# A fused attention, expert and dense kernel: dense slices issued between the last experts, with every engine's order written out

## The chip, the cores and the metric

The kernel runs on one NeuronCore of a Trainium2 chip. The metric is the device time of one execution in microseconds (us). A core has a matrix engine (PE in the profile; its weight loads are PEld), a vector engine (DVE), an activation engine (ACT), a general engine (POOL) that issues the indirect transfers, and a queue engine (SP) that issues all other transfers. Each engine works through its own instructions in their order; semaphores hold an instruction until what it needs is there.

## What is computed

Three layers follow one another on 1536 tokens of width 512, all in 32-bit floats:

```python
a = softmax([local window scores, block scores])       # 2 batches, 8 heads, 768 positions
x = (a @ [v, block means of v]).reshape(1536, 512)
skip = x @ w_skip <= 0                                 # about half of the tokens
e = argmax(x @ w_gate)                                 # one of 8 experts for each other token
x[~skip] += gate * (relu(x @ w1[e]) @ w2[e])           # 512 -> 1024 -> 512
h = x @ w_in                                           # 512 -> 2048, the dense layer
g = where(h >= 1, h, where(h <= -1, 0, (h + 1)**2 / 4))
out = g @ w_out                                        # 2048 -> 512
```

## The kernel before

**Stages.** Attention and routing run first. Routing scatters the tokens into lists in device memory (`xf`), by expert; the skipped tokens lie at its head, so the first 512 rows (`EARLY`) need no expert. Then eight expert steps p = 0 to 7 run, and then the dense layer in three chunks of 512 tokens.

**An expert step.** The tokens of step p are a block of `ROOM[p]` rows: 64 for p = 0 and 6, 32 for the others, and 160 for one large expert (`BIG`, here p = 4), which is worked as a block of 32 rows and one of 128. For a block, `xs` transposes the rows on PE and copies the result on ACT; `as_` multiplies with w1 on PE (for 32 rows on four quarters of the array's columns at once, each with another quarter of the hidden values, L888) and applies relu on ACT (L890); `ts` transposes the hidden values on PE and copies them on ACT (L899); `bs` multiplies with w2 on PE (L906); `ys` adds the result into the rows on DVE, one instruction for each part of the result in PSUM (L914): four for a block of 32 rows, two for one of 64. `put` scatters the rows back on POOL. For the 128 rows the steps are `mx`, `ma`, `mt`, `mb` (L920, L229, L235, L240). PE's pipeline is ts(p), as_(p+1), xs(p+2), bs(p).

**Expert weights.** Each expert has 4 MB, loaded in four transfers by `fetch` (L129) on SP into one of four pairs of slots.

**The dense layer.** Its weights come in 16 slices f. `ff_fetch` loads the 64-bit words of a slice (1 MB, two transfers, L1012 and L1014) into one of four 8 KB buffers (pool `b8`); three DVE instructions (L1024, L1027, L1030, "bits") make floats of them; ACT rounds them to a high part (L1045, "high"); DVE forms the low part (L1046, "low"). The high part of an odd slice and the hidden values of experts share the tile tag `h`. For a chunk and slice, `mm1` is 12 matmuls of 512 columns (L1080), `act` makes g (in chunk 0 four ACT instructions, L1092 to L1095, then a DVE add, L1100, an ACT cast, L1105, and a DVE subtract, L1106), and `mm2` is 12 matmuls (L1121 to L1123). PE's order is mm1(i), mm2(i-1), mm1(i+1). In total there are 48 such pairs, 1152 matmuls. The first chunk's 512 rows come by four loads on SP (L857) into the ring of row buffers, issued during steps 4 and 5, and are transposed by `turn0` on PE (L219) and split in two parts on ACT and DVE (L224, L225).

**Order.** In attention, all engines issue as written. In the expert and dense stages of the kernel before only SP and POOL do; the order on PE, DVE and ACT is the planner's, steered by priorities (`SHIFT`) and by a work list from which `fill` takes a given number of conversion steps at given places (`FILLS`, `FFILLS`).

Of the kernel before, what the change touches and what calls it, by code (L numbers as in the profile page):

```python
# [30 lines left out]
SLOTS = (("00", "01"), ("02", "03"), ("10", "11"), ("13", "12"))  # L31
FFSLOTS = ("00", "01", "02", "03", "10", "11", "12", "13")
NRAW = 4
FILLS = ((0, 0, 0), (0, 0, 0), (0, 0, 0), (0, 0, 2), (2, 2, 2, 2), (2, 1, 1), (1, 1, 2))
LAST = 2
FFILLS = ((2, 1, 2), (2, 0, 2))
SHIFT = {'bits': 6, 'round': -57, 'act': -1, 'add': -97, 'g': 8, 'y': 18, 'x': -8, 't': 6, 'turn': 0}
YLAST = 4
PLACES = {4: 0, 5: 2, 6: 1, 7: 3}
# [3 lines left out]
def tile_net(ctx, tc, q, k, v, w_skip, w_gate, w1, w2, w_in, w_out, out):  # L43
# [12 lines left out]
    xnext = iter(xring * NT)  # L56
# [30 lines left out]
    wg = cp.tile([128, 4, 9], F32, name="wg")  # L87
    placei = cp.tile([1, 18], I32, name="placei")
# [33 lines left out]
    def fetch(p, c):  # L122

        n = 2 if c < 2 else 4
        if c % 2 == 0:
            tag = "w" + SLOTS[p % 4][c // 2]
# [5 lines left out]
    def work_list():  # L132

        def convert(f):
            for step in range(3):
                yield lambda: ff_bits(f, step)
            yield lambda: ff_round(f)

        for f in range(3):
            yield from convert(f)  # L140
            if f:
                for c in (2 * f - 2, 2 * f - 1):
                    yield lambda: st["turn0"](c)
        for f in range(3, NF):
            yield from convert(f)
            if f == YLAST:
                yield lambda: st["ylast"]()

    work = work_list()

    def fill(n):

        for _ in range(n):
            w = next(work, None)
            if w is not None:
                w()

    moves, puts = [], []

    def apart(d, xg, others=()):  # L160

        for o, x in moves:
            if x is not xg and all(x is not y for y in others):
# [14 lines left out]

    @contextmanager
    def shift(name):  # L180
        now = tc.cur_priority
        d = SHIFT.get(name, 0)
        tc.cur_priority = max(0, now + d)
        yield
        tc.cur_priority = now + (tc.cur_priority - max(0, now + d))
# [59 lines left out]
    def attention(actx):  # L245
# [579 lines left out]
        for f in range(2, NRAW):  # L825
            ff_fetch(f)
# [10 lines left out]
        late()  # L837
        fb_a(0, (2, 3))
# [6 lines left out]
        for c in range(4):  # L845
            fetch(3, c)
        get(BIG[0])
# [5 lines left out]
    reads = []  # L853

    def get_slots(c):
        xg = next(xnext)
        d = nc.sync.dma_start(out=xg.bitcast(I32), in_=xf[128 * c:128 * c + 128])  # L857
        if 128 * c < EARLY:
            apart(d, xg, reads)
            reads.append(xg)  # L860
        nc.vector.tensor_copy(out=perm[:, c:c + 1], in_=xg[:, 513:514].bitcast(I32))
        return xg


    def experts(mctx):
# [7 lines left out]
        def xs(key):  # L873
            n, xg = st["n", key], st["x", key]
            tp = ps.tile([128, 4, n], F32, tag="tp", name="tpx", bufs=3)
# [3 lines left out]
            with shift("x"):  # L879
                nc.scalar.copy(out=xT, in_=tp)  # L880
# [11 lines left out]
        def ts(key):  # L892
            h, n = st.pop(("h", key)), st["n", key] // 16
            tp = ps.tile([128, n, 128], F32, tag="tp", name="tph", bufs=3)
# [3 lines left out]
            with shift("t"):  # L898
                nc.scalar.copy(out=hT, in_=tp)  # L899
# [37 lines left out]
        more = {0: (5,), 1: (6,), 3: (7,)}  # L937

        xslot = {}

        def get_slot(c):
            xslot[c] = get_slots(c)

        def turn0(c):
# [4 lines left out]
            with shift("turn"):  # L949
                x128(xslot[c], xh[:, :, a], xl[:, :, a], ps.tile([128, 4, 128], F32, tag="tp", name="tps", bufs=3))  # L950

        st["turn0"] = turn0
        early = {p: [] for p in range(E)}
        for c in range(4):
            early[4 + c // 2].append(lambda c=c: get_slot(c))

# [339 lines left out]
```

## Time and profile before

| what | value |
| --- | --- |
| time, median of 3 runs (lowest to highest) | 488.2 us (486.65 to 488.48) |
| time of the profiled execution | 488.5 us |
| its span, first to last instruction | 486.8 us |
| mean granted clock of PE | 0.965 of full |
| PE busy | 455.6 us, 94% of the span |
| DVE busy | 273.7 us, 56% |
| ACT busy | 207.9 us, 43% |
| transfers | 77.19 MB, 159 GB/s over the span |

Times in the profile count from the first instruction. PE's busy time is modelled and runs over when matmuls are pipelined, so how fast PE goes is read from the starts of its instructions. In the rows below, "x16" after a matmul counts hardware instructions; a 32-bit float matmul is two of them. "[5.52 <-DMA x]" says that the engine was idle for 5.52 us before, and what ended it. The granted clock is shown as a share of 2.4 GHz.

### The profile page before, as it was taken

The page shows a single profiled execution, that of the slowest core. Times are in us where ns is not written, and L with a number is a line of the kernel's source. Part 1 is how long each engine was busy: PE and PEld are TensorE (multiplying, and loading weights), DVE is VectorE, ACT ScalarE, POOL GpSimd, SP SyncE. Part 2 cuts the span into 40 slices and gives each one's busy share as a digit, 9 for nine tenths or more (in the row PEclk, how much of TensorE's full clock was granted, in tenths as well). Part 3 has the DMA queues.
Part 4 walks back from the last instruction along what each step waited for, and adds up shares of the span by engine and source line. Part 5 has one row for each costly group of instructions (what it writes and reads, how often), then busy time and mean ns, then how long its engine had stood idle before and what let it go on. Part 6 is the DMA issues. An engine that isn't in the chain of part 4 may idle for free.

```text
span 486.8 us, 8032 instructions
## 1 busy us (share of the span) xinstructions
PE 455.6 (94%) x3010; PEld 332.3 (68%) x3010; DVE 273.7 (56%) x629; ACT 207.9 (43%) x418; POOL 70.6 (15%) x143
## 2 busy tenths in 40 slices
PE   6889999988979995999999999999999999999993
PEld 3567777765434341557778888888888888888882
DVE  3666575785611457599999954433334453333341
ACT  4556555451112122357767765433333443333341
POOL 7001940222330300130000000300000030000003
PEclk9999998995989999699999999999999999999998
DMA  9999999989999999444556600200000020000002
GB/s 196 198 216 194 196 174 230 376 306 374 391 365 398 385 396 380 141 140 140 183 197 224 241 1 25 86 0 1 0 2 0 1 86 0 2 0 1 0 0 94
DMA packets 77104, 77.19 MB, mean 159 GB/s; under 512 B 50606, under 2 KB 58830, under 8 KB 76672
## 3 DMA queue, kind: packets, MB, share of 16 engines
q1 hardware_dynamic: 74176, 68.33, 48.2%
q0 software_dynamic: 2880, 8.25, 4.6%
q8 instruction: 26, 0.43, 0.4%
q14 instruction: 22, 0.18, 0.1%
HBM read 69.44 MB, written 7.76 MB: 159 GB/s over the span
## 4 chain that ended last, share of the span: by engine, by line
issue 42%; PE 29%; DMA 11%; DVE 10%; POOL 5%; SPq 1%; ACT 1%; POOLq 0%; DVEq 0%; ACTq 0%
PE hf L1080 7%; DMA xf<-x,ids 5%; DMA vraw<-in_v_dram 3%; PE s L395 3%; PE o L1121 3%; PE o L1123 2%; PE o L1122 2%; POOL vraw L323 2%; PE hp L229 2%; PE xo L425 2%; POOL out_dram L1133 1%; PE yp L240 1%; PE pt L407 1%; DVE x L914 1%; SPq L303 1%
## 5 line engine op out<-in xcount | busy, mean ns | idle before, releaser
L1080 PE MATMUL hf<-xh,ffw 128*128 128x512 f32 x384 | 126.6, 390 | 0.0
L1080 PEld LDWEIGHTS hf<-xh,ffw 128*128 128x128 f32 x384 | 72.1, 188 | 16.1 <-issue 0.8
L1121 PE MATMUL o<-ffw,g 128*128 128x512 f32 x192 | 76.3, 397 | 0.1
L1122 PE MATMUL o<-ffw,g 128*128 128x512 f32 x192 | 75.5, 393 | 0.0
L1080 PE MATMUL hf<-xl,ffw 128*128 128x512 f32 x192 | 74.9, 390 | 0.0
L1123 PE MATMUL o<-ffw,g 128*128 128x512 f32 x192 | 70.2, 391 | 0.0
L1090 ACT ACTIVATE c<-c,scal 128x512 f32<-128x512 f32 x32 | 23.2, 724 | 74.5 <-DVE c L1089 72.2
L1100 DVE TENSOR_TENSOR hf<-hf,c 128x512 f32<-128x512 f32 x48 | 33.5, 698 | 37.6 <-ACT hf L1098 36.1
L1133 POOL DMA_INDIRECT out_dram<-ob,perm x12 | 11.7, 974 | 247.3 <-DVE ob L1132 162.5
L1106 DVE TENSOR_TENSOR g<-hf,g 128x512 fp32r<-128x512 f32 x48 | 33.1, 690 | 23.4 <-ACT g L1105 23.3
L1089 DVE TENSOR_SCALAR c<-hf 128x512 f32<-128x512 f32 x32 | 22.1, 692 | 40.1 <-PE hf L1080 40.1
L1105 ACT CAST g<-hf 128x512 fp32r<-128x512 f32 x48 | 28.2, 587 | 37.9 <-DVE hf L1100 37.8
L400 ACT ACTIVATE p<-s,nm 128x120 f32<-128x120 f32 x96 | 26.7, 361 | 37.1 <-DVE nm L397 19.8
L1121 PEld LDWEIGHTS o<-ffw,g 128*128 128x128 f32 x192 | 36.1, 188 | 8.8 <-ACT g L1105 1.2
L1123 PEld LDWEIGHTS o<-ffw,g 128*128 128x128 f32 x192 | 36.0, 188 | 8.6 <-DVE g L1106 0.3
L1080 PEld LDWEIGHTS hf<-xl,ffw 128*128 128x128 f32 x192 | 36.1, 188 | 7.5
L1122 PEld LDWEIGHTS o<-ffw,g 128*128 128x128 f32 x192 | 36.1, 188 | 7.0
L914 DVE SCALAR_TENSOR_TENSOR x<-yp,x 32x512 f32<-32x512 f32 (+1 forms) x28 | 20.8, 744 | 10.5 <-PE yp L906 9.6
L395 PE MATMUL s<-pb 64*64 64x120 f32 x384 | 25.7, 275 | 0.0
L397 DVE TENSOR_REDUCE nm<-s 128x4 f32<-128x480 f32 x24 | 15.7, 653 | 15.4 <-PE s L395 12.4
L395 PEld LDWEIGHTS s<-pb 64*64 64x64 f32 x384 | 20.1, 136 | 5.4 <-issue 5.4
L1045 ACT CAST ffw<-cv 128x1024 fp32r<-128x1024 f32 x16 | 16.6, 1046 | 13.3 <-DVE cv L1030 11.4
(221 smaller groups left out, 643.4 us busy)
## 6 DMA issues: line engine op xcount, KB each, us to landing
w<-in_moe_w_dram SPq DMA_DIRECT2D x32, 1024.0 KB, 15.3
raw<-in_moe_w_in_dram SPq DMA_DIRECT2D x16, 512.0 KB, 4.2
raw<-in_moe_w_out_dram SPq DMA_DIRECT2D x16, 512.0 KB
x<-xf SPq DMA_DIRECT2D x12, 264.0 KB, 5.2
raw<-in_k_dram SPq DMA_DIRECT2D x16, 192.0 KB
raw<-in_q_dram SPq DMA_DIRECT2D x16, 192.0 KB, 5.0
vraw<-in_v_dram SPq DMA_DIRECT2D x4, 768.0 KB, 7.8
vw<-in_v_dram SPq DMA_DIRECT2D x13, 192.0 KB, 6.2
```

Source lines behind the costliest of these rows:

```text
L395: nc.tensor.matmul(s[a, u], tq[a, j], tk[a, j], start=False, stop=u == 3)
L400: nc.scalar.activation(out=p[:, u], in_=s[:, u], func=AF.Exp, bias=nm[:, u:u + 1], scale=1.0)
L914: nc.vector.scalar_tensor_tensor(out=xg[0:n, 0:512], in0=yp[a], scalar=xg[0:n, 512:513], in1=xg[0:n, 0:512], op0=ALU.mult, op1=ALU.add)
L1080: nc.tensor.matmul(hp, w[:, 128 * kk:128 * kk + 128], a[:, kk], start=(n == 0), stop=(n == 11))
L1089: nc.vector.tensor_scalar(out=c, in0=hp, scalar1=-1.0, scalar2=1.0, op0=ALU.max, op1=ALU.min)
L1090: nc.scalar.activation(out=c, in_=c, func=AF.Square, bias=half, scale=0.5)
L1100: nc.vector.tensor_tensor(out=hp, in0=hp, in1=c, op=ALU.add)
L1105: nc.scalar.copy(out=gh, in_=hp)
L1106: nc.vector.tensor_tensor(out=gl, in0=hp, in1=gh.bitcast(F32), op=ALU.subtract)
L1121: nc.tensor.matmul(ops[ch][t], gh[:, a], hi, start=(f == 0), stop=False)
L1122: nc.tensor.matmul(ops[ch][t], gh[:, a], lo, start=False, stop=False)
L1123: nc.tensor.matmul(ops[ch][t], gl[:, a], hi, start=False, stop=(f == NF - 1))
```

## The change

- The large expert moves from step 4 to step 5 (`BIG`, `ROOM`, `PLACES`, `SLOTS`).
- The first 512 rows come by one load into a `b8` buffer, issued on SP after the routing and before the weights of step 3 (`get_rows`); a second small transfer takes the 512 output places. The loads of raw slices 2 and 3, which stood before the weights of step 3, move back: slice 2 to step 1, slice 3 to step 4.
- `bs` puts the four parts of a 32-row block in two places of PSUM instead of four, and `ys` adds two parts instead of four.
- The indices of `put` have twelve columns of their own instead of four rotating buffers.
- Slices 0 and 1 are converted in step 3, and the first chunk's rows are turned in step 4, where the first mm1 also goes. Five dense slices' mm1 and four mm2 are issued between steps 4 and 7; weights of steps 6 and 7 are loaded between the raw slices.
- In the expert and dense stages every engine issues in the order of the text (`manual_schedule()` without an argument); `feed` becomes a generator that stops after mm1 and `act`, after `split`, and after mm2.

```diff
-BIG = (4,)
-ROOM = (64, 32, 32, 32, 160, 32, 64, 32)
+BIG = (5,)
+ROOM = (64, 32, 32, 32, 32, 160, 64, 32)
...
-        ids = cp.tile([128, 1], I32, tag="ids", name="ids", bufs=4)
+        ids = next(putids)
...
-        for f in range(2, NRAW):
-            ff_fetch(f)
...
         late()
+        get_rows()
...
+    def get_rows():
+
+        t = st["rows"] = b8.tile([128, 4, 512], F32, tag="b8", name="rows")
+        v = xf[0:EARLY].rearrange("(t p) c -> p t c", p=128)
+        for out, c in ((t.bitcast(I32), slice(0, 512)), (perm[:, 0:4].unsqueeze(2), slice(513, 514))):
+            d = nc.sync.dma_start(out=out, in_=v[:, :, c])
+            apart(d, t)
+
...
-            for c in range(n // 16):
+            m = n // 16
+            for c in range(m):
                 for f, a in enumerate(sides(n)):
-                    nc.tensor.matmul(yp[a], hT[:, c, a], wx[p, 1][:, n // 16 * f + c], start=c == 0, stop=c == n // 16 - 1)
+                    nc.tensor.matmul(yp[sides(n)[f % 2]], hT[:, c, a], wx[p, 1][:, m * f + c], start=c == 0 and f < 2,
+                                     stop=c == m - 1 and f >= 128 // n - 2)
             st["y", key] = yp
 
...
-            with shift("y"):
-                for a in sides(n):
-                    nc.vector.scalar_tensor_tensor(out=xg[0:n, 0:512], in0=yp[a], scalar=xg[0:n, 512:513],
-                                                   in1=xg[0:n, 0:512], op0=ALU.mult, op1=ALU.add)
+            for a in sides(n)[0:2]:
+                nc.vector.scalar_tensor_tensor(out=xg[0:n, 0:512], in0=yp[a], scalar=xg[0:n, 512:513],
+                                               in1=xg[0:n, 0:512], op0=ALU.mult, op1=ALU.add)
             put(key)
...
+        big = BIG[0]
         xs(0)
         as_(0, 0)
         xs(1)
         st.pop("beyond")()
-        for p in range(E - 1):
-            last = p + 2 == E
+        for p in range(big):
             ts(p)
-            if p in BIG:
-                mt((p, 1))
+            if p < 2:
+                fetch(p + 4, 0), fetch(p + 4, 1)
             if p:
                 ys(p - 1)
-                if p - 1 in BIG:
-                    put((p - 1, 1))
-            for o in more.get(p, ()):
-                get(o)
-            if p + 4 < E:
-                fetch(p + 4, 0), fetch(p + 4, 1)
-            n = iter(FILLS[p])
-            fill(next(n))
+            if p in (1, 2):
+                get(p + 5)
+            if p == 3:
+                convert(0)
+                convert(1)
+            if p == 4:
+                turn0(0), turn0(1)
+                bs(4, 4)
+                turn0(2), turn0(3)
+                st.pop("rows")
+                ff_fetch(3)
+                for c in range(4):
+                    fetch(6, c)
+                ys(4)
+                g = feed()
+                next(g), next(g), next(g)
+                ff_fetch(4)
             as_(p + 1, p + 1)
-            fill(next(n))
-            if p + 1 in BIG:
+            if p + 1 == big:
                 for f in range(2):
-                    ma((p + 1, 1), p + 1, f)
-            for f in early[p]:
-                f()
-            if not last:
-                xs(p + 2)
-                if p + 2 in BIG:
-                    mx((p + 2, 1))
+                    ma((big, 1), big, f)
+                break
+            xs(p + 2)
+            if p + 2 in BIG:
+                mx((p + 2, 1))
             bs(p, p)
-            if last:
-                ys(p)
-                ts(p + 1)
-            fill(next(n))
-            if p in BIG:
-                mb((p, 1), p)
-                if last:
-                    put((p, 1))
-                fill(next(n))
-            if p + 4 < E:
+            if p < 2:
                 fetch(p + 4, 2), fetch(p + 4, 3)
-            if p == E - 2:
-                ff_fetch(NRAW), ff_fetch(NRAW + 1)
-        bs(E - 1, E - 1)
-        st["ylast"] = lambda: ys(E - 1)
-        fill(LAST)
+            if p == 1:
+                ff_fetch(2)
+        ts(big)
+        mt((big, 1))
+        xs(6)
+        convert(2)
+        bs(big, big)
+        mb((big, 1), big)
+        convert(3)
+        ys(big)
+        put((big, 1))
+        ff_fetch(5)
+        fetch(7, 0), fetch(7, 1)
+        st["late"] = "h"
+        next(g)
+        as_(6, 6)
+        next(g)
+        next(g)
+        ts(6)
+        bits(4)
+        ff_fetch(6)
+        fetch(7, 2), fetch(7, 3)
+        high(4), low(4)
+        next(g)
+        bs(6, 6)
+        xs(7)
+        next(g)
+        ys(6)
+        next(g)
+        bits(5)
+        ff_fetch(7)
+        next(g)
+        as_(7, 7)
+        next(g)
+        high(5), low(5)
+        next(g)
+        ts(7)
+        bits(6)
+        high(6), low(6)
+        next(g)
+        bs(7, 7)
+        next(g)
+        next(g)
+        bits(7)
+        ys(7)
+        bits(8, (0, 1))
+        st["next"], st["auto"] = 8, 1
+        for _ in g:
+            pass
 
...
-    def ff_bits(f, step):
+    def bits(f, steps=range(3)):
...
-        if step == 2:
-            raw64.pop(f)
-            if NRAW <= f < NF - 2:
-                ff_fetch(f + 2)
-
-    def ff_round(f):
+                raw64.pop(f)
+                if 5 < f < NF - 2:
+                    ff_fetch(f + 2)
+
+    def high(f):
 
         g = f // 2
...
-        nc.vector.tensor_tensor(out=lo, in0=uf, in1=hi.bitcast(F32), op=ALU.subtract)
+        nc.scalar.copy(out=ffw[g][:, f % 2, 0:4:2], in_=cv[f].bitcast(F32))
+
+    def low(f):
+
+        w = ffw[f // 2][:, f % 2]
+        nc.vector.tensor_tensor(out=w[:, 1:4:2], in0=cv.pop(f).bitcast(F32), in1=w[:, 0:4:2].bitcast(F32),
+                                op=ALU.subtract)
+
+    def convert(f):
+        bits(f), high(f), low(f)
...
+
+        def split(ch, f, hp, c, between=None):
+            nc.vector.tensor_tensor(out=hp, in0=hp, in1=c, op=ALU.add)
+            if between is not None:
+                between()
...
         for i, (ch, f) in enumerate(seq):
             hp = mm1(ch, f)
-
-            act(ch, f, hp, FFILLS[min(i, len(FFILLS) - 1)])
+            c = act(ch, f, hp)
+            yield
+            n = st.get("next", NF + 1)
+            auto = "auto" in st
+            if auto:
+                runs(n - 1, high)
+            split(ch, f, hp, c, (lambda: runs(n, lambda f: bits(f, (2,)))) if auto else None)
+            if auto:
+                runs(n - 1, low)
+                runs(n + 1, lambda f: bits(f, (0, 1)))
+                st["next"] = n + 1
+            yield
...
     with ExitStack() as mctx:
-        with tc.manual_schedule(engines={EngineType.SP, EngineType.Pool}):
+        with tc.manual_schedule():
             experts(mctx)
-            feed()
```

## Rows read from the trace of the kernel before

**Rows 1.** Engine busy time by stretches of the expert and dense stages.
```profile
core 0: us, PE busy (x) PEld busy (x) DVE busy (x) ACT busy (x) POOL busy (x), PEclk, DMA share, GB/s
138.00:142.00 4.00, 4.00 (x14) 1.22 (x12) 0.05 (x1) 0.00 (x0) 0.12 (x1) 0.57 1.02 374
...
163.00:189.00 26.00, 25.02 (x138) 10.10 (x126) 14.06 (x19) 4.51 (x9) 3.79 (x4) 1.00 1.04 391
189.00:195.00 6.00, 0.48 (x4) 0.07 (x2) 3.19 (x5) 2.59 (x3) 0.37 (x1) 0.83 0.95 347
195.00:203.00 8.00, 7.81 (x37) 4.36 (x38) 2.88 (x9) 1.91 (x5) 1.35 (x1) 0.50 0.44 136
...
210.00:283.00 73.00, 72.86 (x326) 57.45 (x325) 70.18 (x88) 52.78 (x80) 3.66 (x2) 1.00 0.54 187
283.00:478.00 195.00, 195.00 (x871) 160.75 (x870) 80.34 (x117) 75.10 (x124) 8.77 (x9) 1.00 0.04 13
```

**Rows 2.** Timeline of PE: its longest wait, and its last matmul (start, duration, instruction).
```profile
194.96 1.94 PE L219 MATMUL tps<-ident,x 128*128 128x128 f32 x8 [5.52 <-DMA x<-xf]
...
479.02 0.39 PE L1123 MATMUL o<-ffw,g 128*128 128x512 f32 x1
```

**Rows 3.** Timeline of the queue engine SP: the four loads of the first rows.
```profile
180.40 18.10 SPq L857 DMA_DIRECT2D x<-xf  x4
```

**Rows 4.** Timeline of PE through the expert steps 0 to 2.
```profile
136.64 0.79 PE L877 MATMUL tpx<-ident,x 64*128 64x64 f32 x8 [2.30 <-DMA x<-xf,re]
...
146.22 3.65 PE L906 MATMUL yp<-w,hT 128*64 128x512 f32 x16
149.80 0.44 PE L896 MATMUL tph<-ident,h 128*128 128x128 f32 x2
150.17 1.93 PE L888 MATMUL hp<-w,xT 128*32 128x256 f32 x32
152.03 0.43 PE L877 MATMUL tpx<-ident,x 32*128 32x32 f32 x4
152.39 1.92 PE L906 MATMUL yp<-w,hT 128*32 128x512 f32 x16
154.25 0.44 PE L896 MATMUL tph<-ident,h 128*128 128x128 f32 x2
```

**Rows 5.** DVE's groups, 120 to 290 us: busy, mean ns of one, idle before.
```profile
L1030 DVE SCALAR_TENSOR_TENSOR cv<-raw,cv 128x1024 int32<-128x1024 int32 x16 | 19.5, 1219 | 0.1
L1027 DVE SCALAR_TENSOR_TENSOR cv<-raw,cv 128x1024 int32<-128x1024 int32 x16 | 19.5, 1224 | 0.3
L1046 DVE TENSOR_TENSOR ffw<-cv,ffw 128x1024 fp32r<-128x1024 f32 x16 | 19.5, 1218 | 1.0 <-ACT ffw L1045 0.8 <-issue 0.2
L914 DVE SCALAR_TENSOR_TENSOR x<-yp,x 32x512 f32<-32x512 f32 x24 | 17.8, 743 | 3.6 <-PE yp L906 2.9
L1024 DVE TENSOR_SCALAR cv<-raw 128x1024 int32<-128x1024 int32 x16 | 11.0, 686 | 3.3 <-DMA xf<-x,si 2.1 <-DMA raw<-in_moe_w_out_dram 1.2
L1100 DVE TENSOR_TENSOR hf<-hf,c 128x512 f32<-128x512 f32 x14 | 9.7, 696 | 0.2
```

**Rows 6.** ACT's groups in the same stretch, in the same columns.
```profile
L1045 ACT CAST ffw<-cv 128x1024 fp32r<-128x1024 f32 x16 | 16.6, 1046 | 13.3 <-DVE cv L1030 11.4 <-PE hp L229 1.9
L1095 ACT ACTIVATE c<-c,scal 128x512 f32<-128x512 f32 x14 | 10.2, 730 | 0.1
...
L1105 ACT CAST g<-hf 128x512 fp32r<-128x512 f32 x14 | 8.2, 588 | 12.1 <-DVE hf L1100 12.1
...
L890 ACT ACTIVATE h<-hp 128x256 f32<-128x256 f32 x6 | 2.3, 384 | 18.9 <-PE hp L888 17.3 <-issue 1.6
```

**Rows 7.** Timeline of ACT around two conversions and the relu behind them.
```profile
189.45 1.99 ACT L1045 CAST ffw<-cv 128x1024 fp32r<-128x1024 f32 x2 [8.44 <-DVE cv L1030]
193.66 0.60 ACT L890 ACTIVATE h<-hp 128x512 f32<-128x512 f32 x1 [2.22 <-DVE ffw L1046]
```

**Rows 8.** PE's group of the 128-row second matmul, 136 to 210 us.
```profile
L240 PE MATMUL yp<-w,hTm 128*128 128x512 f32 x16 | 7.4, 605 | 0.0
```

**Rows 9.** The chain of waits in the dense stage: start, time on the chain, what.
```profile
290.68 0.44 PE tpf L1062 x4
...
293.89 2.73 PE hf L1080 x12
```

More of the change, by code (lines that the diff above doesn't have):

```diff
@@ L1 @@
-from contextlib import ExitStack, contextmanager
+from contextlib import ExitStack
 import concourse.bass as bass
@@ L26 @@
 NEARLY = 4
-BIG = (4,)
-ROOM = (64, 32, 32, 32, 160, 32, 64, 32)
+BIG = (5,)
+ROOM = (64, 32, 32, 32, 32, 160, 64, 32)
 LISTS = 1536
 EOFF = 28 * CAP + 8 * LISTS
[L31 to L39, printed above, removed]
+SLOTS = (("00", "01"), ("02", "03"), ("10", "11"), ("13", "12"), ("00", "01"), ("02", "03"), ("10", "11"), ("00", "01"))
+FFSLOTS = ("13", "12", "02", "03", "10", "11", "00", "01")
+XORDER = (0, 1, 2, 3, 4, 5, 6, 0, 1, 2, 3, 4, 5) + (6, 0, 1, 2, 3, 5, 4, 6, 0) + (1, 2, 3, 4, 5, 6, 0, 1)
+PLACES = {4: 2, 5: 0, 6: 1, 7: 3}
 @with_exitstack
@@ L55, in tile_net @@
     xring = [xp.tile([128, XW], F32, name=f"x{i}") for i in range(7)]
-    xnext = iter(xring * NT)
+    xnext = iter([xring[i] for i in XORDER])
     dr = ctx.enter_context(tc.tile_pool(name="dr", bufs=1, space=DRAM))
@@ L87, in tile_net @@
     wg = cp.tile([128, 4, 9], F32, name="wg")
+    idsall = cp.tile([128, 12], I32, name="ids")
+    putids = iter([idsall[:, i:i + 1] for i in range(12)])
     placei = cp.tile([1, 18], I32, name="placei")
@@ L130, in fetch, with apart @@
                           .rearrange("p e k f -> p (e k) f"))
[L132 to L156, printed above, removed]
     moves, puts = [], []
-    def apart(d, xg, others=()):
+    def apart(d, xg):
         for o, x in moves:
-            if x is not xg and all(x is not y for y in others):
+            if x is not xg:
                 tc.declare_no_dep(d.ins, o.ins, reason="the blocks have different tokens")
@@ L846, in attention @@
             fetch(3, c)
+        get(4)
         get(BIG[0])
@@ L874, in xs @@
             n, xg = st["n", key], st["x", key]
-            tp = ps.tile([128, 4, n], F32, tag="tp", name="tpx", bufs=3)
+            tp = ps.tile([128, 4, n], F32, tag=st.get("late", "tp"), name="tpx", bufs=3)
             for kk in range(4):
@@ L878, in xs @@
             st["xT", key] = xT = wk.tile([128, 4, n], F32, tag="xT", name="xT", bufs=3)
-            with shift("x"):
-                nc.scalar.copy(out=xT, in_=tp)
+            nc.scalar.copy(out=xT, in_=tp)
         def as_(key, p):
@@ L897, in ts @@
             st["hT", key] = hT = wk.tile([128, n, 128], F32, tag="hT", name="hT", bufs=3)
-            with shift("t"):
-                nc.scalar.copy(out=hT, in_=tp)
+            nc.scalar.copy(out=hT, in_=tp)
         def bs(key, p):
@@ L948, in turn0 @@
             xh, xl = xTs[0]
[L949 to L955, printed above, removed]
+            x128(st["rows"][:, c], xh[:, :, a], xl[:, :, a], ps.tile([128, 4, 128], F32, tag="tp", name="tps", bufs=3))
+        big = BIG[0]
         xs(0)
@@ L1015, in ff_fetch @@
         raw64[f] = t
-    def ff_bits(f, step):
-        if step == 0:
-            cv[f] = st["wk"].tile([128, 2, 512], I32, tag="h" if f % 2 else "cv", name="cv", bufs=2 if f % 2 else 1)
-        t, o = raw64[f], cv[f]
-        with shift("bits"):
+    def bits(f, steps=range(3)):
+        for step in steps:
+            if step == 0:
+                odd = f % 2
+                cv[f] = st["wk"].tile([128, 2, 512], I32, tag="h" if odd else "cv", name="cv", bufs=2 if odd else 1)
+            t, o = raw64[f], cv[f]
             if step == 0:
@@ L1140, in feed, with runs @@
         seq = [(ch, f) for ch in range(NC) for f in range(NF)]
+        def runs(f, *fs):
+            for g in fs:
+                g(f) if f < NF else None
         for i, (ch, f) in enumerate(seq):
             hp = mm1(ch, f)
-            act(ch, f, hp, FFILLS[min(i, len(FFILLS) - 1)])
+            c = act(ch, f, hp)
[10 more added lines that the diff above has]
+            yield
             if ch + 1 < NC:
@@ L1148, in feed @@
                 if f >= NF - 4:
-                    turn(ch + 1, f - NF + 4, range(4))
-                    parts(ch + 1, f - NF + 4)
+                    kk = f - NF + 4
+                    turn(ch + 1, kk, range(4))
+                    get_perm(4 * (ch + 1) + kk, xin[ch + 1][kk])
+                    parts(ch + 1, kk)
             if i and i + 2 < len(seq):
                 mm2(*seq[i - 1])
+            yield
         a, b, c = seq[-3:]
```

57 lines of the change are left out of this document (16 added, 41 removed).

## The prediction

> **What bounds the kernel now.** I read the busy time by stretches first, then PE's timeline, then the groups of DVE and ACT. From 210 us on PE sets the time: between 283 and 478 it is never idle and DVE is busy for 80 of 195 us; between 210 and 283 PE is still full although DVE works 70.2 of 73 [rows 1]. A dense matmul starts every 2.73 / 12 = 0.2275 us [rows 9], so 1152 take 262.1; with 32 transposes of the later chunks (0.44 for four [rows 9], 3.5 together) the dense layer costs PE 265.6 us. PE's last matmul ends at 479.4 [rows 2], and the profiled time is 488.5, so 9.1 lies behind and around. That part stays.
>
> The expert steps are PE's too. In steps 0 to 2 one instruction group follows the other without a gap [rows 4]; the transfers run at full share in that stretch, but no row there has PE waiting for a weight. The losses are elsewhere: PE stands still for 5.5 us before 194.96, until a load of the first rows lands [rows 2]; SP issued those four loads over 18.1 us [rows 3], behind the last weights. Then PE runs at half clock, 1.2 GHz, from 195 to 203 [rows 1], where 8 us do the work of 4. So 9.6 us can be won here. A smaller loss is a half-clock stretch at 138 to 142 after a wait of 2.3 us for gathered rows [rows 1, 4]; nothing in the change touches it, since the weights still fill the queues there. I take 0; were that wait to vanish with its half clock, 4.0 us would come off.
>
> **Part by part. The first rows.** Their load now stands on SP before the weights of step 3, in a time when the queue has nothing else to issue, and is used only in step 4. The 5.5 and 4.1 us go. The 1 MB moved ahead replaces 2 MB of raw slices, so the weights of steps 3 to 5 land no later. The second, small transfer has 512 pieces; nothing waits for its places until the first output, so it is hidden. Separate index columns for put cost nothing and remove waits of DVE that PE doesn't see.
>
> **bs on two places.** A 64-row block already runs eight matmuls on two places: 3.65 us. A 32-row block runs eight of the same width on four: 1.92 [rows 4]. After the change the 32-row blocks use two as well, so each bs costs PE 1.73 more; steps 1 to 5 and 7 have one. What it saves is two instructions of 0.74 on DVE [rows 5], 12 in all, 8.9 us on an engine that isn't the bound before 210. Lower bound of the price: 0, if the places didn't matter; upper bound 1.73; I take 1.7, since the two rows differ in nothing else.
>
> The Trainium skill, TensorEngine Tiling (Array Packing), section "Overview" (Theoretical Speedup), gives up to 4 times for 32 columns and up to 2 times for 64, which speaks against this edit. By it the price would be the whole of 1.92, and the sum below 0.9 us longer; the rows show a ratio of 1.9, so nearly that.
>
> **Steps 1 to 3, as written.** bs of step 0 ends at 149.8 [rows 4]; without the planner's filling some 0.5 later, at 150.3. A step is ts, as_, xs, 2.6 us (149.80 to 152.39 [rows 4]), and a bs of 3.6: steps 1 and 2 end at 156.5 and 162.7. Step 3 on PE is 2.6, the large block's transposes 0.6, and 3.6: done at 169.5. But in the text the conversions of slices 0 and 1 stand in step 3 before the relu of as_(4). DVE first does ys(2), which waits for bs(2) at 162.7: two of 0.74 and the index, 1.9 with gaps. Then, with 0.69, 1.22, 1.22 for bits, 1.22 for low [rows 5] and 1.05 for high [rows 6]: bits(0) 3.2, high(0) 1.1, low(0) 1.3, bits(1) 3.2, high(1) 1.1, relu 0.45 and a signal 0.2: ts(4) can start at 162.7 + 12.4 = 175.1. ACT has the relu queued behind high(1), and PE has ts(4), turn0 and bs(4) queued behind that relu. PE stands still for 5.6 us. The trace has this in small: a relu on ACT starts 2.2 us late behind two conversions, held until a low part is done [rows 7]. Bounds: 0, if the relu got past, and 7.3, if PE had no cover from the longer bs(3). I take 5.6.
>
> The Trainium skill, TensorE: Matmul & The Clock Gate, section "Architectural detail: the array is 16× 32×32, not 1× 128×128", calls the queues of ACT and DVE strictly first in, first out. By that rule the relu can't pass; without it this sum would be 5.6 shorter; rows 7 agree with the rule.
>
> **The clock.** Idle times of 2.3 and 5.5 us were each followed by 1.2 GHz [rows 1, 2, 4]. For 5.6 us I take 2 us of loss; the bounds are 0 and the 4.1 seen at 195.
>
> **Step 4.** From 175.1: ts 0.4, two turn0 0.9 (with the row copies still queued on ACT, to 176.5), bs(4) 3.6, two turn0 0.9: 181.0. mm1(0) needs the last low part of the rows: two casts of 0.59 and a subtract of 0.69 behind the transposes, 1.7 us in which PE waits. mm1 2.73: 185.4, and with the clock 187.4. Call that M.
>
> **After M.** PE's own work up to the end of mb is as_(5) 1.9, ma 6.9, three transposes 1.7, bs(5) 3.6, mb 6.9 (7.4 busy [rows 8] less the last one's tail): M + 21.0. Then to the first matmul of mm2(5): mm1(1) to (6) and mm2(0) to (4), 11 of 2.73, with as_(6), bs(6), as_(7), bs(7) and transposes, 43.4, and 0.3 of small waits: M + 64.7. DVE must by then have g(5). In the text convert(3) stands behind mb's addition, so bits(3) can't start before M + 21.9 although DVE is free for 7 us before. From there DVE and ACT take turns, each link behind the one before: bits(3), high(3), four activations (0.7 each [rows 6]), relu, cast, subtract to M + 31.5; bits(4), high(4), activations, add, cast, subtract to 40.9; ys(6), bits(5) to 45.8; g(3) and low(5) to 49.5; bits(6), high(6), activations, g(4) to 58.8; bits(7), ys(7), two thirds of bits(8) to 65.7; add, last third, subtract: g(5) at M + 68.4. PE waits 3.3 us in mm2(5), done at M + 70.7. Then each iteration asks DVE for an add, three bits, a low part and a subtract, 0.70 + 3.13 + 1.22 + 0.69 with gaps 5.9, against PE's 5.46: some 0.45 is lost in each of six iterations, 2.9 with the first, until the last slice is converted. The raw slices land in time: each load is issued at least 5 us before its bits. Bounds for this stage: 1.5 us, what the stage loses before (from 210 to 479.4 are 269.4 us for 265.6 and 2.3 of expert work), and 6.2; I take 6.2, because the order is fixed.
>
> **The sum.** Left after M + 70.7 are 996 matmuls, 226.6, the transposes, 3.5, and 2.9: PE ends at M + 303.7 = 491.1. With 9.1: 500.2 against 488.5; the run lies 0.3 above the median. Forecast 500.
>
> **Rivals.** *The order costs nothing.* The relu of step 4 isn't held, and DVE keeps up behind M: one mechanism, conversions that don't stand in the way of what PE needs. Then ts(4) starts at 169.5, M is 179.8, and PE ends at M + 297.5 = 477.3: 486.4, not slower. For it: DVE is busy only 14 of 26 us between 163 and 189 [rows 1], so there is room for both conversions. Against it: rows 7, and that ys(2) ties their start to bs(2). It decides from the point where high(1) is done before 169.5, 5.6 us earlier than I have it. With the 4.0 of the gathered rows it would be 482.
>
> *The places of bs cost nothing.* Then steps 1 and 2 end 3.5 earlier, bs(4) and bs(5) save 1.7 each (bs(3) and bs(7) lie under other waits): 493. The two rows of bs speak against it.
>
> *The rows come late all the same,* behind weights as now: up to 5.5 us more in step 4, 505. Against it: 12 MB of weights stand behind them, not before.
>
> **How the numbers follow.** My forecast, with its own range 494 to 504: 0.66. Free places: 0.07. Late rows or a longer half clock: 0.05. Order free, 486.4: 0.15. Order free and the gather earlier, 482: 0.07. Half a per cent, 2.4 us, is about what a measurement of this kernel can tell from no change. Slower: 0.78; same: 0.15; faster: 0.07. The range 487 to 505 leaves out the fastest case and about half of the one before it.
>
> **What would show it.** ACT's relu of step 4 some 5 us after as_(4), behind two L1045-like casts; PE idle for 5 to 6 us before the transposes of that step, and half clock after; bs of 32 rows at 3.6 us; no wait for the first rows; PE waiting on a subtract of g around the sixth slice. The forecast is wrong if PE runs through step 3, or if mm1(0) starts before 178 us.

## The result and the profile after

The changed kernel takes 494.4 us, median of 4 runs (493.9 to 497.0), against 488.3 (486.7 to 488.7) of the kernel before: 6.0 us more by the medians. The ratio over all runs is 1.0141, 95% interval 1.0105 to 1.0177, so 1.4% slower. Forecast was 500.0, slower, in a range of 487 to 505. The profiled execution is the slowest of the four, 497.0 us with a span of 495.3.

PE's timeline of the changed kernel, steps 1 to 4, answers to [rows 2, 4]. M is again the end of mm1(0), here 184.46.

```profile
150.65 3.63 PE L873 MATMUL yp<-w,hT 128*32 128x512 f32 x16
154.21 0.44 PE L863 MATMUL tph<-ident,h 128*128 128x128 f32 x2
...
160.36 0.44 PE L863 MATMUL tph<-ident,h 128*128 128x128 f32 x2
160.73 1.93 PE L855 MATMUL hp<-w,xT 128*32 128x256 f32 x32
...
163.54 3.63 PE L873 MATMUL yp<-w,hT 128*32 128x512 f32 x16
172.09 0.69 PE L863 MATMUL tph<-ident,h 128*128 128x128 f32 x2 [4.92 <-ACT h L857]
172.58 1.91 PE L182 MATMUL tps<-ident,rows 128*128 128x128 f32 x8
174.42 4.62 PE L873 MATMUL yp<-w,hT 128*32 128x512 f32 x16
178.97 1.09 PE L182 MATMUL tps<-ident,rows 128*128 128x128 f32 x8
180.79 0.50 PE L1080 MATMUL hf<-xh,ffw 128*128 128x512 f32 x1 [0.73 <-ACT xh L187]
181.63 0.50 PE L1080 MATMUL hf<-xl,ffw 128*128 128x512 f32 x1 [0.34 <-DVE xl L188]
```

No line waits for a transfer of the first rows. In its place stands an idle time of 4.92 us ahead of step 4's transposes, released by the relu (L857). A 32-row bs takes 3.63 us, where [rows 4] have 1.92. ACT's timeline says why the relu was late:

```profile
165.22 1.04 ACT L1037 CAST ffw<-cv 128x1024 fp32r<-128x1024 f32 x1 [4.01 <-DVE cv L1026]
170.71 1.04 ACT L1037 CAST ffw<-cv 128x1024 fp32r<-128x1024 f32 x1 [4.45 <-DVE cv L1026]
171.66 0.38 ACT L857 ACTIVATE h<-hp 128x256 f32<-128x256 f32 x1
```

The relu's input, the L855 group of as_(4) at 160.73, was done at 162.7. The relu began at 171.66, right behind the second of two casts, and ACT was idle for 4.01 and 4.45 us before these, waiting for DVE's bits. The windows, which answer to [rows 1], show the clock and the DVE stretch:

```profile
core 0: us, PE busy (x) PEld busy (x) DVE busy (x) ACT busy (x) POOL busy (x), PEclk, DMA share, GB/s
138.00:142.00 4.00, 3.66 (x21) 1.38 (x18) 0.00 (x0) 0.75 (x2) 1.82 (x2) 1.00 0.96 352
...
167.00:172.00 5.00, 0.17 (x2) 0.00 (x0) 3.82 (x5) 1.29 (x3) 0.21 (x1) 0.76 1.05 381
172.00:176.00 4.00, 3.90 (x14) 2.37 (x16) 3.85 (x6) 2.23 (x6) 0.89 (x1) 0.50 0.85 300
...
250.00:283.00 33.00, 32.22 (x141) 25.95 (x140) 32.69 (x38) 24.80 (x37) 0.00 (x0) 1.00 0.68 236
```

After the idle time PE runs at 1.2 GHz from 172 to 176. From 250 to 283 DVE is busy for 32.69 of 33 us, and PE still for 32.22. The wait for a part of g in mm2(5), the second matmul of the sixth slice, is short in PE's timeline:

```profile
250.89 0.50 PE L1119 MATMUL o<-ffw,g 128*128 128x512 f32 x1 [0.41 <-ACT g L1104]
251.23 0.40 PE L1120 MATMUL o<-ffw,g 128*128 128x512 f32 x1
252.00 0.50 PE L1121 MATMUL o<-ffw,g 128*128 128x512 f32 x1 [0.37 <-DVE g L1105]
```

The matmul before the first of these started at 250.09. By the starts, at 0.2275 us a matmul, the two waits are 0.57 + 0.54 = 1.1 us.

### The profile page after: what moved, and what is told of

The parts are those of the page before. It is cut to its first block, busy times and chain, and to the rows that moved or that the text cites. A ratio compares the mean times of both kernels' runs of the same rounds, so it can differ in the third digit from the quotient of the medians.

```text
span 495.3 us, 7993 instructions
## 1 busy us (share of the span) xinstructions
PE 462.0 (93%) x3010; PEld 333.0 (67%) x3010; DVE 265.3 (54%) x613; ACT 208.7 (42%) x418; POOL 68.0 (14%) x143
## 4 chain that ended last, share of the span: by engine, by line
issue 36%; PE 36%; DVE 8%; DMA 7%; SPq 4%; POOL 4%; ACT 2%; ACTq 1%; POOLq 0%; DVEq 0%
PE hf L1080 8%; PE yp L873 4%; SPq L266 3%; PE hp L855 3%; DMA w<-in_moe_w_dram 3%; PE o L1119 3%; PE o L1121 2%; PE o L1120 2%; PE s L358 2%; PE hp L192 2%; POOL vraw L286 2%; PE xo L388 2%; DMA vw<-in_v_dram 2%; DMA vraw<-in_v_dram 2%; POOL out_dram L1131 2%
## 5 line engine op out<-in xcount | busy, mean ns | idle before, releaser
L1119 PE MATMUL o<-ffw,g 128*128 128x512 f32 x192 | 76.7, 399 | 1.1 <-ACT g L1104 1.1
L1120 PE MATMUL o<-ffw,g 128*128 128x512 f32 x192 | 75.5, 393 | 0.0
L1121 PE MATMUL o<-ffw,g 128*128 128x512 f32 x192 | 75.1, 391 | 0.4 <-DVE g L1105 0.4
L1089 ACT ACTIVATE hf<-hf,scal 128x512 f32<-128x512 f32 x32 | 21.2, 662 | 85.2 <-DVE c L1088 85.2
L1131 POOL DMA_INDIRECT out_dram<-ob,perm x12 | 11.7, 974 | 229.7 <-DVE ob L1130 227.0
L873 PE MATMUL yp<-w,hT 128*32 128x512 f32 (+1 forms) x128 | 30.1, 613 | 0.0
L1037 ACT CAST ffw<-cv 128x1024 fp32r<-128x1024 f32 x16 | 16.6, 1039 | 28.3 <-DVE cv L1026 28.3
L1042 DVE TENSOR_TENSOR ffw<-cv,ffw 128x1024 fp32r<-128x1024 f32 x16 | 19.6, 1222 | 10.0 <-ACT ffw L1037 10.0
```

Of the source, the lines that this page charges most:

```text
L873: nc.tensor.matmul(yp[sides(n)[f % 2]], hT[:, c, a], wx[p, 1][:, m * f + c], start=c == 0 and f < 2, stop=c == m - 1 and f >= 128 // n - 2)
L1119: nc.tensor.matmul(ops[ch][t], gh[:, a], hi, start=(f == 0), stop=False)
L1120: nc.tensor.matmul(ops[ch][t], gh[:, a], lo, start=False, stop=False)
L1121: nc.tensor.matmul(ops[ch][t], gl[:, a], hi, start=False, stop=(f == NF - 1))
L1131: d = nc.gpsimd.indirect_dma_start(out=out[:, :], out_offset=bass.IndirectOffsetOnAxis(ap=perm[:, 4 * ch + t:4 * ch + t + 1], axis=0), in_ ...
```

## The experiments

The kernels did not all run on one chip, so each is told by its ratio to the kernel before on its own chip and its 95% interval. Within a trace, lengths are counted from ts(0), the first transposes of hidden values, since what lies ahead of it differs by some us between executions; the last section has the waits there. "Front" is ts(0) to M, "back" is M to PE's last matmul. The changed kernel has 184.46 - 141.66 = 42.8 and 488.05 - 184.46 = 303.6, together 346.4; the kernel before, in which mm1(0) comes later, has 335.6 together. Work is left out in none. No run separates the other parts of the change, above all the large expert's move and the dense slices between the experts.

| kernel | ratio (interval) | front | back | sum |
| --- | --- | --- | --- | --- |
| changed | 1.0141 (1.0105 to 1.0177) | 42.8 | 303.6 | 346.4 |
| conversions spread | 1.0014 (0.9991 to 1.0038) | 35.7 | 303.6 | 339.3 |
| four places everywhere | 1.0106 (1.0083 to 1.0129) | 39.1 | 305.8 | 344.8 |
| spread, four places in steps 1, 2 | 0.9937 (0.9915 to 0.9959) | 32.3 | 303.6 | 335.9 |
| before, rows alone | 1.0121 (1.0090 to 1.0153) | - | - | 344.8 |
| before, two places alone | 1.0105 (1.0079 to 1.0132) | - | - | 342.4 |
| changed, planner's order | 1.0405 (1.0381 to 1.0428) | 53.5 | 300.0 | 353.5 |
| all three edits | 0.9939 (0.9919 to 0.9959) | 29.3 | 305.8 | 335.1 |
| two edits behind the large expert | 1.0194 (1.0162 to 1.0226) | 43.1 | 305.1 | 348.2 |
| all three, less late DVE work | 0.9814 (0.9799 to 0.9830) | 29.2 | 301.6 | 330.8 |
| same, first mm1 covered | 0.9791 (0.9776 to 0.9807) | 29.8 | 298.5 | 328.2 |
| before, rows alone, earlier list | 1.0085 (1.0065 to 1.0106) | - | - | 341.8 |

**Conversions spread.**

```diff
+            if p in (3, 4):
+                low(p - 3)
             if p:
                 ys(p - 1)
...
-            if p == 3:
-                convert(0)
-                convert(1)
+            if p == 1:
+                bits(0)
...
+            if p == 2:
+                bits(1)
...
             bs(p, p)
+            if p in (2, 3):
+                high(p - 2)
```

> The changed kernel, with the conversions of slices 0 and 1 spread out: bits(0) in step 1, bits(1) in step 2, high(0) after bs(2), high(1) after bs(3), low(0) and low(1) behind the transposes of steps 3 and 4. Nothing else differs. Theory: in the changed kernel PE stands still for 4.92 us in step 4 because ACT's relu of that step is written behind high(1), and the stretch at half clock after it costs some 2 us more. Then both go: no idle time of over 1 us before the transposes of step 4, full clock from 165 to 180, mm1(0) at about 174.8 instead of 180.8, and 494.4 - 6.9 = 487.5 us. Rival, the order costs nothing (PE waits for something else there, as a late weight): the idle time stays or moves by a step, 494. Rival, the gain is given back in the chain of conversions behind the large expert: the end of mm1(0) comes 6 us earlier, but the wait in mm2(5) grows by some 3 us or more: 490 to 491.

The front is 7.1 us shorter, the back unchanged. PE's timeline has no idle time ahead of the transposes of step 4, and bs(4) takes 3.63 again:

```profile
164.95 0.44 PE L863 MATMUL tph<-ident,h 128*128 128x128 f32 x2
165.22 1.04 PE L182 MATMUL tps<-ident,rows 128*128 128x128 f32 x8
166.19 3.63 PE L873 MATMUL yp<-w,hT 128*32 128x512 f32 x16
```

So the hold was the position of two conversions in the text, and cost 4.9 us of waiting and 2.2 of clock. Without it the kernel is level with the kernel before: 1.0014, with 1 inside the interval. That doesn't make the hold the only cost: other costs and gains of the change cancel. In the profiled runs this kernel is 3.7 us longer than the kernel before from ts(0) on, and the kernel before lost 3.3 us more ahead of it (from the last 128-row second matmul ahead of the experts to ts(0), 143.84 - 127.23 = 16.6 us against 139.51 - 126.23 = 13.3).

**Four places everywhere.**

```diff
-                    nc.tensor.matmul(yp[sides(n)[f % 2]], hT[:, c, a], wx[p, 1][:, m * f + c], start=c == 0 and f < 2,
+                    nc.tensor.matmul(yp[a], hT[:, c, a], wx[p, 1][:, n // 16 * f + c], start=c == 0, stop=c == n // 16 - 1)
...
-            for a in sides(n)[0:2]:
+            for a in sides(n):
```

> The changed kernel with bs of a 32-row block back on four places of PSUM and ys back on four additions. Theory: two places cost PE 1.7 us for each block. Steps 1 and 2 get 3.5 us shorter, bs(3) only lengthens the idle time, ys(2) is 1.5 longer ahead of the conversions, so ts(4) starts 2.0 earlier; bs(4) is 2 shorter; behind the large expert bs(5) and bs(7) save 3.4 on PE, but ys(5) and ys(7) put 3.0 more on DVE, and the wait in mm2(5) grows from 1.1 to some 6. Sum about -2.6: 491.8 us (490 to 493). Rival, the places of bs cost nothing: bs stays at 3.6 us, and only the additions are left, +1.5 and +3.0: 498 to 499. Rival, DVE has room for the four additions everywhere: -7 and more, 487 or less.

A bs takes 1.92 on PE's timeline; the hold grows to 8.19, as DVE's chain behind ys(2) is longer and PE arrives earlier; the wait in mm2(5) grows to 3.87:

```profile
159.24 1.92 PE L872 MATMUL yp<-w,hT 128*32 128x512 f32 x16
169.35 0.69 PE L863 MATMUL tph<-ident,h 128*128 128x128 f32 x2 [8.19 <-ACT h L857]
...
246.32 0.80 PE L1117 MATMUL o<-ffw,g 128*128 128x512 f32 x1 [3.87 <-ACT g L1102]
246.92 0.63 PE L1118 MATMUL o<-ffw,g 128*128 128x512 f32 x1
```

The front gives 3.7, the back takes 2.2, so the profiled run is 1.5 shorter from ts(0) on. The ratios' intervals overlap: in this order no effect of the places can be told. PE's saving of 1.7 for each of six blocks, 10.3, comes back for the most part: 3.3 in the longer hold, of which 1.5 are additions, and 5.6 behind M, in the longer wait and what follows it. That the places are free on PE is refuted.

**Both, the places in steps 1 and 2 alone.**

```diff
+        def parts_of(key, n):
+
+            return sides(n)[0:4 if key in (1, 2) else 2]
...
-            for a in sides(n)[0:2]:
+            for a in parts_of(key, n):
```

> The changed kernel with both: the conversions of slices 0 and 1 spread over steps 1 to 4 as in the experiment before, and four places of PSUM (and four additions) for steps 1 and 2 alone, where DVE is idle. Theory: the two costs are separate and add up: -6.9 and -3.5, less what DVE's longer additions hold back the low parts of the first rows: M, the end of mm1(0), at about 173.5 instead of 184.4, and the end likewise: 483.5 us (482 to 486), faster than the kernel before. Rival, the conversions of the raw slices wait for DVE or the transfers behind the large expert: M comes early, but the wait in mm2(5) or a wait for weights of step 6 takes it back: 487 or more.

The front falls by another 3.4, twice 1.7, and the back stays: the two costs add up where DVE is idle.

**The rows alone, in the kernel before.**

```diff
-NRAW = 4
+NRAW = 3
...
-        for f in range(3):
+        for f in range(2):
             yield from convert(f)
...
+        get_rows()
...
+            if c == 3:
+                st.pop("rows")
+                ff_fetch(3)
```

> The kernel before with one part of the change alone: the first 512 rows come in one load issued behind the routing into a b8 buffer, raw slice 3 is loaded when the rows are turned, and the four turns follow slice 1 in the work list. Order on PE, DVE and ACT is still the planner's, and bs and the large expert are as before. Theory: the wait of 5.5 us for the first rows and the half clock after it, 4.1 us, go: 488.3 - 9.6 = 478.7 us; with the earlier gather that the changed kernel showed (0.84 instead of 2.30, no half clock) up to 2 less. Rival, the wait moves to what is late next (a raw slice, DVE's subtract of the rows): at least half of it stays, 483 to 485. Rival, the rows were not what held PE: 488.

None of the three expected outcomes was a loss. The wait for the rows is gone, the transposes start at 185.19 instead of 194.96 [rows 2], but PE then waits 5.76 us for a copy of hidden values. PE and ACT there:

```profile
192.21 1.12 PE L218 MATMUL tps<-ident,rows 128*128 128x128 f32 x4 [5.76 <-ACT hT L902]
```

```profile
188.92 1.99 ACT L1041 CAST ffw<-cv 128x1024 fp32r<-128x1024 f32 x2 [8.41 <-DVE cv L1026]
190.82 1.06 ACT L223 CAST xh<-tps 128x512 fp32r<-128x512 f32 x2
191.77 0.38 ACT L902 COPY hT<-tph 128x256 f32<-128x256 f32 x1
```

It is the hold of the changed kernel, a conversion ahead of what PE needs, in the planner's order. But DVE, whose bits the casts wait for, was late too:

```profile
178.05 0.15 DVE L206 SCALAR_TENSOR_TENSOR ids<-vl,x 64x1 int32<-64x1 f32 x1 [5.44 <-DMA xf<-x,ids]
```

It stood idle for 5.44 us until a scatter gave back one of `put`'s four rotating index buffers, and worked without a gap from there to the end of the bits, at 188.89. The kernel before has the same wait (5.41 us before 178.58), but there the rows come later still. The changed kernel gives `put` columns of its own; this run doesn't have them, so what the order alone costs here is not shown.

A second loss follows: at 230.67 and 232.73 mm1 waits 1.82 and 1.32 for a slice's two parts, though the transfers are idle from 214 to 230 (share 0.00); that slice's bits start at 224.57, and DVE was idle for 6.56 us before 218.28. These bits wait for no transfer. That they fall late because the rows take one of four 8 KB buffers isn't shown; the planner's order alone could do it.

**The same, with the work list taken earlier.** By the end of steps 3 and 4 four more conversion steps have been taken, after step 5 one.

```diff
-FILLS = ((0, 0, 0), (0, 0, 0), (0, 0, 0), (0, 0, 2), (2, 2, 2, 2), (2, 1, 1), (1, 1, 2))
+FILLS = ((0, 0, 0), (0, 0, 0), (0, 0, 1), (1, 2, 2), (2, 2, 2, 2), (0, 0, 1), (1, 1, 1))
```

> The run with the rows alone (planner's order, 1.012 of the kernel before), with the work list taken two items earlier in steps 2 to 4, so that slice 1 is converted before the hidden values of step 5 are copied. Theory: in the run with the rows alone the copy of step 5's hidden values stood behind two casts on ACT, 5.8 us of idle time for PE; with those casts done sooner the wait goes, and the rows give some 5 to 9 us: 0.982 to 0.99 of the kernel before. Rival, the planner lets a cast or a low part stand ahead of something else that PE needs: 1.0 or more.

The rival held: the idle time is 5.56 now, at 180.87, behind DVE's subtract of the rows, and the waits at the slice stay (1.82 and 1.33). DVE again stood idle just before, for 5.46 us up to 175.06, for an index buffer of `put`. What list would let the planner use the early rows was not found, and early rows together with index columns were not tried on this text. The planner's order of the changed text, below, has both; there DVE waits for gathers.

**The places alone, in the kernel before.**

```diff
-                    nc.tensor.matmul(yp[a], hT[:, c, a], wx[p, 1][:, n // 16 * f + c], start=c == 0, stop=c == n // 16 - 1)
+                    nc.tensor.matmul(yp[sides(n)[f % 2]], hT[:, c, a], wx[p, 1][:, m * f + c], start=c == 0 and f < 2,
...
-                for a in sides(n):
+                for a in sides(n)[0:2]:
```

> The kernel before with one part of the change alone: bs of a 32-row block on two places of PSUM, ys with two additions. Theory: 1.73 us on PE for each of six blocks. Those of steps 1 to 3 (5.2) only shorten the wait of 5.5 us for the first rows, that of the large expert's step comes half under it; the last two stand on PE's path, one of them at half clock: +4 to +6, 493 us. Rival, PE's price is paid back by the additions that DVE no longer does, since DVE works 70 of 73 us between 210 and 283: 488 (487 to 490). Rival, the places of bs cost PE nothing: 488 or a little less.

Measured 489.05 against 484.43, +4.6 by the medians (ratio 1.0105), in the expected 4 to 6. The wait for the rows falls from 5.5 to 1.76 us: it had covered the first blocks.

**The planner's order on the changed text.**

```diff
-        with tc.manual_schedule():
+        with tc.manual_schedule(engines={EngineType.SP, EngineType.Pool}):
```

> The changed kernel with the written order on SP and POOL alone; on PE, DVE and ACT the planner orders the same text. Theory: the 5 us of idle time and the 2 us at half clock belong to the order as written, where the relu of step 4 stands behind two conversions; the planner lets a relu that is ready go first: 487 to 489 us. Rival, the planner puts the conversions ahead of what PE needs as well (as it did with the hidden values' copy in the run with the rows alone): 494 or more.

The theory fell: 4% slower. The planner keeps the casts ahead of the relu, and puts a small DVE instruction of `put` for a later block ahead of everything; DVE waits for that block's gather. PE and DVE:

```profile
177.87 0.69 PE L863 MATMUL tph<-ident,h 128*128 128x128 f32 x2 [11.01 <-ACT h L857]
```

```profile
165.03 0.15 DVE L170 SCALAR_TENSOR_TENSOR ids<-vl,x 64x1 int32<-64x1 f32 x1 [10.04 <-DMA x<-xf,rl]
165.21 1.52 DVE L881 SCALAR_TENSOR_TENSOR x<-yp,x 32x512 f32<-32x512 f32 x2
172.12 0.15 DVE L170 SCALAR_TENSOR_TENSOR ids<-vl,x 32x1 int32<-32x1 f32 x1 [5.38 <-DMA x<-xf,rl]
```

So the written order as such is no loss; against this one order of the planner it is worth over 2% for this text.

**Two edits behind the large expert; all three edits.** The first moves `convert(3)` and has four places in steps 5 and 7. The second adds the spread conversions and four places everywhere, and moves ys(3) and low(1).

```diff
+            return sides(n)[0:4 if key in (5, 7) else 2]
...
         convert(2)
+        convert(3)
         bs(big, big)
         mb((big, 1), big)
-        convert(3)
```

The second, beside the spread conversions:

```diff
-            for a in sides(n)[0:2]:
+            for a in sides(n):
...
-            if p:
+            if p == 3:
+                low(0)
+            if 0 < p < 4:
                 ys(p - 1)
...
+                low(1)
+                ys(3)
                 ys(4)
                 g = feed()
```

> The changed kernel with two edits behind the large expert alone: conversion 3 ahead of bs(5) and the large expert's second matmul, and four places and additions for bs(5) and bs(7). The hold in step 4 stays. Theory: it was DVE's chain, which starts behind the large expert's addition, that took back what four places gave in the run with four places everywhere; with the chain started sooner -1.1 for the wait and -3.4 for the two blocks remain: 494.4 - 4.5 = 489.9 us, PE's end at M + 299. Rival, the chain isn't what holds PE there, and the additions cost what the places give: 494, PE's end at M + 303 or later.

> The changed kernel with conversions 0 and 1 spread over steps 1 to 4, conversion 3 ahead of the large expert's second matmul instead of behind its addition, four places and four additions in every bs of 32 rows, and low(1), ys(3) and ys(4) behind the low parts of the first rows. Theory: DVE's chain behind the large expert starts some 10 us sooner, so DVE has room for the additions and the wait of 1.1 us in mm2(5) goes. Against the run with the spread conversions and places in steps 1 and 2 (486.0): bs(3) and bs(4) -3.4, less 1 for DVE's low parts, bs(5) and bs(7) -3.4, the wait -1.1: -6.9, 479 us (478 to 482), and the first matmul of mm2(5) at M + 61.5. Rival, DVE is full even so: the wait in mm2(5) stays at 1 us or grows to 4, 483 to 486. Rival, the raw slices' loads are late next, since PE comes to them earlier: a wait of DVE for a load behind M, 483 or more.

Here my own theory fell. The conversion ran 8.7 us earlier after M in the first and 7.7 in the second, yet the back grew to 305.1 and 305.8. In the first, PE waits 3.66 us in mm2(5), and the clock is 0.72 over 244 to 250; in the second it waits 3.64. DVE's timeline of the first shows where the chain begins:

```profile
219.53 1.23 DVE L1031 SCALAR_TENSOR_TENSOR cv<-raw,cv 128x1024 int32<-128x1024 int32 x1
223.05 0.70 DVE L1104 TENSOR_TENSOR hf<-hf,c 128x512 f32<-128x512 f32 x1 [2.30 <-ACT c L1100]
...
237.29 1.23 DVE L1031 SCALAR_TENSOR_TENSOR cv<-raw,cv 128x1024 int32<-128x1024 int32 x1
238.44 3.08 DVE L886 SCALAR_TENSOR_TENSOR x<-yp,x 32x512 f32<-32x512 f32 x4
...
243.47 0.70 DVE L1104 TENSOR_TENSOR hf<-hf,c 128x512 f32<-128x512 f32 x1
```

DVE stands idle for 2.30 us until mm1(3) has been through ACT; only from there the chain runs to mm2(5), with waits of 0.26 to 1.31 us of DVE for ACT. The lead of the early conversion is lost in that gap, and ys(7) stands with 3.08 us in the last piece. bs(5) comes before the piece: its 1.7 is won; bs(7) and ys(7) lose 1.7 and 1.5 to the wait. From the changed kernel's 303.6: -3.4 on PE, +1.7 + 1.5 in the wait, and some 2 of clock, 305.

**All three, less late DVE work; and the first mm1 covered.**

```diff
+            return sides(n)[0:2 if key == 7 else 4]
...
         bits(5)
+        bits(6, (0, 1))
...
-        bits(6)
+        bits(6, (2,))
```

> The run with all three edits, with two changes behind the large expert: bs(7) and ys(7) on two places and two additions again, and two thirds of bits(6) ahead of the third slice's split, in a gap of 2.3 us that the trace shows on DVE there. Theory: the wait in mm2(5) is a chain on DVE that starts at the end of mm1(3) and not at the large expert's addition: bits(6), low parts, bits(7), ys(7), bits(8), two splits. The edits take 1.5 and 1.9 from it and give PE back 1.7, so the wait of 3.8 and the half clock behind it, 2.2, go, for 1.7 more on PE: PE's end falls from M + 305.8 to M + 301, and the time from 0.994 to 0.984 of the kernel before (480.5 where that takes 488.4). Rival, the chain hangs on the large expert's addition or on a late raw slice: the wait stays over 2 us, 0.990 or more.

Right in place and size: 0.9814 against 0.984, back 301.6 against 301. The two edits weren't tried one by one. No wait in mm2(5) is left; PE goes from mm1(6) into it at the usual step:

```profile
230.48 0.39 PE L1093 MATMUL hf<-xh,ffw 128*128 128x512 f32 x1
230.71 0.39 PE L1132 MATMUL o<-ffw,g 128*128 128x512 f32 x1
230.94 0.39 PE L1133 MATMUL o<-ffw,g 128*128 128x512 f32 x1
231.17 0.39 PE L1134 MATMUL o<-ffw,g 128*128 128x512 f32 x1
```

> As the run beside it, and as_(5) ahead of mm1(0). Theory: the 1.1 us for which mm1(0) waits for the last low part of the rows are covered by as_(5): 1 us less, 0.982 of the kernel before. Rival, the weights of step 5 haven't landed by then: PE waits for them instead, the same or 1 to 3 us more.

```diff
                 g = feed()
-                next(g), next(g), next(g)
-                ff_fetch(4)
             as_(p + 1, p + 1)
+            if p == 4:
+                next(g), next(g), next(g)
+                ff_fetch(4)
```

Measured on the same chip 474.8 against 475.8 without it, and 485.0 for the kernel before. as_(5) stands in the gap, no weight is late:

```profile
163.22 1.93 PE L855 MATMUL hp<-w,xT 128*32 128x256 f32 x32
165.09 0.50 PE L1094 MATMUL hf<-xh,ffw 128*128 128x512 f32 x1
```

This version beats both kernels: the kernel before by 2.1%; by the two ratios the changed one by 1 - 0.9791 / 1.0141 = 3.5%.

## Why the prediction was right, step by step

- **First rows.** Right: no wait for them, and the early load is hidden. That alone is a loss under the planner (rows alone, 1.0121): the 9.6 us counted for it could not come out there, since other waits lay under the wait for the rows. One of them is DVE's 5.4 us for `put`'s index buffers, which the prediction called a wait that PE doesn't see; with the early rows it stands at the head of the chain that PE waits for.
- **Gathered rows.** Taken as untouched, 0. The profiled run waited 0.84 instead of 2.30 and had full clock, so steps 1 and 2 end 2.3 earlier than predicted (154.2 and 160.4). Whether the change does it isn't shown: eight profiled runs of its written order waited 0.84 to 1.89, four of the kernel before and its variants 1.55 to 2.60.
- **bs on two places.** Right: 3.63 for 3.65. Of the 10.4 us that six blocks cost, the kernel before would have hidden part under its wait for the rows.
- **The hold in step 3.** Right in place and mechanism, 4.92 for 5.6. From the end of bs(2) to ts(4) the conversions take 11.7 for 12.4; the step after, from ts(4) to M, is 12.4 for 12.3. [rows 7] did not show this mechanism: there ACT was idle for 2.22 us until a low part on DVE, so that relu waited for the subtract and not in ACT's queue. The relu of the changed kernel, right behind its cast, does.
- **The clock.** 2 us taken; the spread conversions give back 7.1, 4.9 of it the wait, so 2.2.
- **After M.** This is the term that was mis-sized: "PE waits 3.3 us in mm2(5)" and 2.9 for iterations in which DVE asks 5.9 us of PE's 5.46, 6.2 together. Measured: 1.1, and nothing behind it. g(5) came at M + 67.5, 0.9 before its predicted time, and PE reached mm2(5) at M + 65.9, 1.2 after the predicted M + 64.7. From 254.85 to 281.88 the add of g starts six times on DVE, so an iteration takes 27.0 / 5 = 5.4 us, not 5.9, and PE's 5.46 hide it. PE's end still is at M + 303.6 for 303.7, and that is luck, by losses that weren't predicted: the 1.2 of the late arrival, 1.2 at 291.6 (transposes of chunk 1, behind a low part), 1.1 at 483.4 (the last parts of g), and some 1.5 in small pieces.
- **The sum.** 500.2 against 497.0 in the profiled run, 3.2 off: 2.3 from the gathered rows and 0.7 from the hold. The profiled run is the slowest; against the median of 494.4 the sum is 5.8 off, so the forecast loss of some 12 us was about twice the measured 6.0. The chance of 0.78 for slower rested on the hold, and the spread conversions bear that out: without it the two kernels are even.

The rival by which the places cost nothing is refuted by the 1.92 and 3.63 of two runs, the one of late rows by the trace of the changed kernel. The rival by which the order costs nothing was wrong for this text, but close to what the text could have been: 486.4 was its price, and the spread order, with the places as predicted, measures 1.0014, some 489. Open is why the planner's order fails with early rows; only three of its orders were seen, two in which DVE waits for an index buffer and one in which it waits for gathers.

## What to carry to other kernels

Where the order is written by hand, place each conversion behind the last thing that the next step of the bound engine needs from ACT and DVE, and start it as soon as its buffer is free; moving two conversions alone took the change from 1.014 to 1.001, and its order together with the places of the partial sums to 0.979. A lead that an engine wins is kept only up to the next point at which it must wait for the bound engine: look for the last such wait and move work from behind it to ahead of it. Weigh an instruction's price on two engines by place: in these runs four partial sums paid where DVE was idle, and not where it ran full.

## What was not expected of the hardware

- **The clock fell after small waits.** Ahead of the first expert's transposes, PE waited 0.84 us in five profiled runs, and the way from them to ts(0) took 5.3 us. In six it waited 1.31 to 2.60, and it took 7.0 to 7.4, at a granted clock of 0.79 over 130 to 138 in one with 1.31, against 1.00 over 130 to 138 in one with 0.84. The planner's order of the changed text waited 4.91 and took 7.6. One run waited 1.55 and took 5.5 at 1.00, so the wait's length alone doesn't decide it.
- **DVE's instructions overlap.** In the changed kernel an add of 0.70 us starts at 249.51 and the next instruction, which doesn't use its result, at 250.12, 0.09 before the add's end; one that needs the result before it starts some 0.03 after. The prediction laid the six instructions of an iteration end to end, 5.74 us, and with gaps 5.9; they took 5.4. The Trainium skill, Perfetto Trace Analysis, section "Optimizing Scalar/DVE Operations", says that the write-acknowledgement half of the access overhead in a profiled duration overlaps with the next instruction; the starts agree that there is an overlap, here of 0.09 us:

```profile
249.51 0.70 DVE L1099 TENSOR_TENSOR hf<-hf,c 128x512 f32<-128x512 f32 x1
250.12 1.22 DVE L1026 SCALAR_TENSOR_TENSOR cv<-raw,cv 128x1024 int32<-128x1024 int32 x1
251.26 0.68 DVE L1105 TENSOR_TENSOR g<-hf,g 128x512 fp32r<-128x512 f32 x1
```
